# A pool of their own for the MoE's moving tiles, beginning at 64 modulo 128 bytes

## The chip, the cores and the metric

The kernel runs on one core of one Trainium2 chip. The metric is the device time of one execution in microseconds (us), and its median over runs is what versions are compared by. A profiled execution shows every instruction with its start and duration; its span runs from the first instruction to the last.

In the tables, PE is TensorE's matmul stream, PEld its weight loads, DVE is VectorE, ACT is ScalarE, POOL is GpSimd, and SP is the engine whose queue issues the transfers. A phase, in this document, is the start of a tile in its partition's bytes, modulo 128.

## What is computed

A linear attention with a decaying state, and behind it a two-layer network with a leaky rectifier of a slope per channel.

```python
batch, n_heads, seq, head_dim = (4, 8, 768, 48)
for t in range(S):
    cur = einsum('bhd,bhe->bhde', u * k[t], v[t])
    y[t] = einsum('bhd,bhde->bhe', r[t], state + cur)
    state = w * state + einsum('bhd,bhe->bhde', k[t], v[t])
x = y as (3072 tokens, 384)
h = x @ w_in                        # 384 -> 2048
g = maximum(h, 0) + alpha * minimum(h, 0)
out = g @ w_out                     # 2048 -> 384
```

All is float32.

## The kernel before

The sequence is cut into 6 chunks of 128 positions. A chunk of all 4 batches is 512 tokens, the moving width of the network (`NT`). The heads are taken in 4 pairs. The attention of a pair and a chunk is a burst of some hundred small matmuls in float32 (lines 543, 550, 569, 579; the first chunk has its own, 410 to 473): they stream `raw` (the scaled r), `base` (the masked scores) and `v` with 48 or 64 columns, in several parts of the array side by side.

The network (MoE in the code's names) runs over 96 steps, one for each chunk and each of 16 blocks of 128 hidden channels. Its matmuls are in the rounded float32 type, and each factor is split in two, a rounded high part and the rest: `xh`, `xl` for the input, `gh`, `gl` for the hidden values, `wh`, `wl` for the weights. A product is the sum of high by high, high by low and low by high. So a step has 9 matmuls of 128x512 on line 628 (`m_in`: three blocks of 128 input rows, each by the three products) and 9 on line 661 (`m_out`: three products, each into the three output banks `acc`). Between them lie four operations: ScalarE copies the bank to `g` (line 636), VectorE applies the slope (637), ScalarE rounds it to `gh` (640), and VectorE subtracts for `gl` (641). `m_out` of a step runs three steps behind its `m_in` (`MLAG`). In the last product of `m_out` the moving tile is `gl`, and what follows is as a rule the next `m_in`, which begins with `xh` and `wh`. The input tiles are written by lines 361 (`xh`) and 362 (`xl`).

The order of the instructions is fixed when the program is built: `Plan` places each piece by a rank and by modelled durations, and every engine gets its instructions in that order. The addresses have no part in it.

Tiles come from pools that fill a partition from the bottom up, in the order in which the pools are opened, and within a pool by name in the order of first use. The pool `const` holds the tables and all weights, `wk` all else. `sb(shape, name, bufs)` takes a tile from `wk` and gives it a name with so many buffers in rotation. `first_chunk` uses the buffers named `gl` a second time, as its masked scores in every other pair. `seen_y` is a small target that ScalarE writes (line 592) so that it is known when a bank has been written; two of its elements are used.

In the built program before, the phases are: weights `wh` and `wl` 64, `xh`, `xl` and `gh` 64, `gl` 32, `kk`, `rr`, `T` and `wx` 64, `base` and `wraw` 32, `raw` and `g` 0, `v` and `o` 96.

Of the kernel before, what the change touches and what calls it, by code (L numbers as in the profile page):

```python
# [8 lines left out]
F32 = mybir.dt.float32  # L9
# [58 lines left out]
class Plan:  # L68
# [12 lines left out]
    def add(self, eng, us, fn, r=(), w=(), rank=0.0, kb=0.0):  # L81
        p = Piece(eng, us, fn, r, w, rank, kb)
        for ref, wr in p.uses:
            b, part = ref if isinstance(ref, tuple) else (ref, None)
            log = self.log.setdefault(b, [])
            for other, opart, owr in log:
                if other is not p and (wr or owr) and (part is None or opart is None or part == opart):
                    p.after.add(other)
            log.append((p, part, wr))
        self.pieces.append(p)  # L90
        return p
# [85 lines left out]
def rwkv_prelu_kernel(ctx: ExitStack, tc, rk, vkr, wP, uP, u, wall, alpha, w, r_all, k_all, v_all, oT):  # L177
    nc = tc.nc

    const = ctx.enter_context(tc.tile_pool(name="const", bufs=1))  # L180
    pools = ctx.enter_context(ExitStack())
    wk = pools.enter_context(tc.tile_pool(name="wk", bufs=1))
    ps = pools.enter_context(tc.tile_pool(name="ps", bufs=1, space=bass.MemoryType.PSUM))
    part = nc.dram_tensor("part", (2, NK, 128, NT), F32, kind="Internal").ap()
# [3 lines left out]
    plan = Plan()  # L188
    add = plan.add

    def sb(shape, name, bufs, dt=F32):
        return plan.buf(lambda: wk.tile(shape, dt, name=name, bufs=bufs), name, bufs)

    def pb(shape, name, bufs=1):
        return plan.buf(lambda: ps.tile(shape, F32, name=name, bufs=bufs), name, bufs)
# [1 line left out]
    def fixed(shape, name, dt=F32):  # L197
        t = const.tile(shape, dt, name=name)
        return plan.buf(lambda: t)
# [165 lines left out]
    def x_tiles(c, q):  # L365
        if q == 0:
            for t, name in ((xh, "xh"), (xl, "xl")):
                t[c] = sb([128, NK, NT], name, 2, F32R)
                top[name] = sb([112, NT], name + "0", 1, F32R)
        return (top["xh"], top["xl"], None) if q == 0 else (xh[c], xl[c], q - 1)  # L370

# [16 lines left out]
    def first_chunk(q):  # L388
        r, k0 = (sb([112, B, L], *(("o", 2) if q == P - 1 else ("raw", 6))) for _ in range(2))
        v, k = sb([128, 2 * B, D], "v", 4), sb([128, 2 * B, D], "kk", 3)  # L390
        n = 2 * B * D
        inputs(0, q, r, k0, v, k, -99 + 0.1 * q)
        first_k.append(k0)
        first_v.append(v)
        if q == P - 1:
            raw_weights(0, -97, [k0])
            raw_weights(1, -95, [v])
        for j, (t, tab) in enumerate(((r, lambda: W[q]()[:, None, 0:L]), (k0, lambda: W[q]()[:, None, L - 1::-1]))):
            add("DVE", 0.72, lambda t=t, tab=tab: nc.vector.tensor_tensor(
                out=t(), in0=t(), in1=tab().broadcast_to([112, B, L]), op=ALU.mult),  # L400
                r=[W[q]], w=[t], rank=10 * q + j - 90)
        cu = sb([128, 2, B], "cu", 2)
        diagonal(q, r, k0, cu, bank, slice(8 * q, 8 * q + 8), (bank, q), 10 * q - 88, -90.2 + q, -51 + q)

        A = [psum() if q % 2 == 0 else pb([128, NT], f"acc{g}") for g in range(2)]

        def scores():
            for b in range(B):
                for g in range(2):
                    nc.tensor.matmul(A[g]()[:, b * L:(b + 1) * L], k0()[half(g), b], r()[half(g), b], start=(b == 0),  # L410
                                     stop=(b == B - 1), skip_group_check=True)

        add("PE", 1.1, scores, r=[r, k0], w=A, rank=10 * q - 90)
        base = [sb([128, B, L], "gl" if q % 2 else "base", 3) for _ in range(2)]
        for g in range(2):
            for b in range(B):
                add("ACT", 0.39, lambda g=g, b=b: nc.scalar.activation(
                    base[g]()[:, b], ident(), AF.Copy, scale=cu()[:, g, b:b + 1]), r=[cu, ident], w=[(base[g], b)],
                    rank=-50.9 + q)
        for g in range(2):  # L420
            add("DVE", 0.75, lambda g=g: nc.vector.copy_predicated(
                base[g](), strict()[:, None, :].broadcast_to([128, B, L]),
                A[g]()[:, :].rearrange("p (b t) -> p b t", b=B)), r=[strict, A[g]], w=[base[g]],
                rank=10 * q - 76 + g)
        y = psum()

        def out():
            for b in range(B):
                for g in range(2):
                    rows, x = (slice(0, HI) if g == 0 else half(g)), g * B + b  # L430
                    nc.tensor.matmul(y()[rows, b * L:(b + 1) * L], v().rearrange("p x e -> p (x e)")[  # L431
                        :, x * D:x * D + rows.stop - rows.start], base[g]()[:, b], start=b == 0,
                        stop=b == B - 1, skip_group_check=True)

        add("PE", 1.0, out, r=[v] + base, w=[y], rank=10 * q - 90)
        h, l, kx = x_tiles(0, q)
        if q < P - 1:
            splits(kx, h, l, y, lambda: y()[0:112, :], slice(0, 112), slice(0, NT), [0, 2, 3, 4, 5], 0.6, q - 51.2)
        if q:
            lower(0, q - 1)  # L440
        if q == P - 1:
            for g in range(2):
                splits(kx, h, l, y, lambda g=g: y()[half(g), :], half(g), slice(0, NT), [2 + 2 * g, 3 + 2 * g], 0.6,
                       q - 51.2)

        def state():
            load(k, lambda: nc.sync.dma_start(k().rearrange("p x e -> p (x e)"), vkr[0, q, :, n:2 * n]), 192,
                 -20 + q, [first_v[P - 1]])
            U = psum()
            add("DVE", 0.56, lambda: scale_k(k, wtok, q), r=[wtok], w=[k], rank=0.5 * q - 1)  # L450

            def product():
                kt = k().rearrange("p x e -> p (x e)")
                for b in range(B):
                    for g in range(2):
                        rows, x = slice(HI * g, HI if g == 0 else HI + D), g * B + b
                        nc.tensor.matmul(u_rows(U, 0)[rows, b], kt[:, x * D:x * D + rows.stop - rows.start], v()[:, x],
                                         start=(b == 0), stop=(b == B - 1), skip_group_check=True)

            add("PE", 0.8, product, r=[k, v], w=[U], rank=0.5 * q - 1)  # L460
            T[q] = sb([112, B, D], "T", 9)
            add("ACT", 0.4, lambda t=T[q]: nc.scalar.activation(t(), u_rows(U, 0), AF.Copy), r=[U], w=[T[q]],
                rank=0.5 * q - 1)
        return state
# [13 lines left out]
            cu(), sums()[:, cols].rearrange("p (b g) -> p g b", g=2), AF.Copy), r=[mine], w=[cu], rank=copy_rank)  # L478


    seen_y = fixed([1, 2], "seen_y")
    pairs = [(c, q) for c in range(1, C) for q in range(P)]
    made = {}

# [39 lines left out]
    def burst(i, was, at):  # L524
# [64 lines left out]
        first = add("PE", (0.7 if before else 0.1) + (0.8 if now else 0.1), run, r=uses, w=writes, rank=at)  # L589
        if before:  # L590

            seen = add("ACT", 0.2, lambda: nc.scalar.activation(seen_y(), y[1]()[0:1, L + HI - 1:L + HI + 1], AF.Copy),
                       r=[y[1]], rank=at - 200)
            seen.soon[first] = 0.75
            add("PE", 0.3, lambda: through_scores(1), r=[v0, base0], w=y, rank=at - 200)
# [26 lines left out]
    def m_in(n):  # L622
        c, i = STEPS[n]
        hp = psum("hp", 2)
        for k in range(NK):
            def mm(k=k):
                for j, (a, x) in enumerate(((wh, xh), (wl, xh), (wh, xl))):
                    nc.tensor.matmul(hp()[:, :], a[i]()[:, k], x[c]()[:, k], start=(k == 0 and j == 0),  # L628
                                     stop=(k == NK - 1 and j == 2))

            need = range(NK) if c and k == 0 else (k,)
            add("PE", 0.7, mm, r=[wh[i], wl[i]] + [(t[c], (kx, p)) for t in (xh, xl) for kx in need for p in range(6)],
                w=[hp], rank=n)
        g = sb([128, NT], "g", 3)
        gh, gl = sb([128, NT], "gh", 3, F32R), sb([128, NT], "gl", 3, F32R)
        add("ACT", 0.6, lambda: nc.scalar.activation(g(), hp()[:, :], AF.Copy), r=[hp], w=[g], rank=n - 100)  # L636
        add("DVE", 0.75, lambda: nc.vector.scalar_tensor_tensor(  # L637
            out=g(), in0=hp()[:, :], scalar=alph()[:, i:i + 1], in1=g(), op0=ALU.mult, op1=ALU.max), r=[hp, alph], w=[g],
            rank=n - 100)
        add("ACT", 0.64, lambda: nc.scalar.activation(gh(), g(), AF.Copy), r=[g], w=[gh], rank=n - 100)  # L640
        add("DVE", 0.73, lambda: nc.vector.tensor_tensor(out=gl(), in0=g(), in1=gh(), op=ALU.subtract), r=[g, gh],  # L641
            w=[gl], rank=n - 99)
        gs[n] = gh, gl
# [256 lines left out]
```

## Time and profile before

| | us |
|---|---|
| median of 3 runs | 502.45 |
| least and most of the 3 | 500.54, 502.52 |
| the profiled execution | 498.5 |
| its span, first to last instruction | 496.7 |
| TensorE busy in the span | 477.7 |
| VectorE, ScalarE, GpSimd busy | 322.1, 242.5, 45.1 |

The page divides the span into 40 slices of 12.4 us and gives a digit for each: the share of the slice in tenths in which an engine was busy, and for PEclk the clock that TensorE was granted, in tenths of full speed. A matmul's duration in the profile overlaps the next one's, since matmuls are pipelined; from one start to the next is the time that it holds the array.

### The profile page before, as it was taken

What the parts mean: (1) busy time and instruction counts of PE and PEld (TensorE: products, weight loads), DVE (VectorE), ACT (ScalarE), POOL (GpSimd) and SP (SyncE); (2) the same over time, 40 slices, a digit from 0 to 9 for tenths busy, and PEclk for the clock granted to TensorE, in tenths of its full rate; (3) what the DMA queues carried; (4) which work ended last, traced back from release to release, by engine and by line L of the source; (5) the groups of instructions that cost most, each with busy time, mean ns of one, the idle gap of its engine ahead of it and who ended that gap; (6) DMA issues with size and microseconds to landing.
All of it is one profiled execution on the core that took longest, in us unless ns stands there. A gap on an engine that the chain in (4) does not pass through costs nothing.

```text
span 496.7 us, 11103 instructions
## 1 busy us (share of the span) xinstructions
PE 477.7 (96%) x4563; PEld 390.2 (79%) x4563; DVE 322.1 (65%) x550; ACT 242.5 (49%) x565; POOL 45.1 (9%) x49
## 2 busy tenths in 40 slices
PE   7989878999999999999999999999999999999994
PEld 6857756788888888888888888888888878888883
DVE  7799999999986677656647546747535434333331
ACT  3777557666764455535535635535633333423332
POOL 2000100001312112100311101211000000000000
PEclk9799999999999999999999999999999999999998
DMA  7965575374152253413212213312120000100001
GB/s 220 299 172 189 153 226 196 126 233 161 49 189 90 80 169 100 147 43 83 86 36 86 95 56 84 86 36 70 63 54 1 1 1 1 64 0 2 0 1 68
DMA packets 24888, 47.39 MB, mean 95 GB/s; under 512 B 4096, under 2 KB 12416, under 8 KB 24832
## 3 DMA queue, kind: packets, MB, share of 16 engines
q1 hardware_dynamic: 24832, 46.62, 30.3%
q8 instruction: 38, 0.62, 0.5%
q14 instruction: 18, 0.15, 0.1%
HBM read 37.96 MB, written 6.29 MB: 89 GB/s over the span
## 4 chain that ended last, share of the span: by engine, by line
PE 84%; DVE 8%; ACT 3%; DMA 2%; issue 1%; SPq 0%; DVEq 0%; ACTq 0%
PE acc L661 38%; PE bank L628 36%; PE bank L569 2%; PE bank L579 2%; PE bank L550 2%; PE bank L543 2%; DMA wraw<-wall 1%; DVE wx L333 1%; DVE xl L362 1%; DMA raw<-rk 1%; DVE wl L337 1%; DVE wx L330 1%; DVE g L637 1%; PE acc L473 1%; DVE raw L496 1%
## 5 line engine op out<-in xcount | busy, mean ns | idle before, releaser
L637 DVE SCALAR_TENSOR_TENSOR g<-bank,alph,g 128x512 f32<-128x512 f32 x96 | 72.0, 750 | 110.0 <-ACT g L636 108.5
L636 ACT ACTIVATE g<-bank 128x512 f32<-128x512 f32 x96 | 57.3, 597 | 141.0 <-PE bank L628 139.1
L628 PE MATMUL bank<-xh,wh 128*128 128x512 f32 x288 | 113.6, 395 | 3.4 <-DVE T L605 3.4
L628 PE MATMUL bank<-xh,wl 128*128 128x512 f32 x288 | 112.3, 390 | 0.4 <-DVE wl L337 0.3
L628 PE MATMUL bank<-xl,wh 128*128 128x512 f32 x288 | 112.1, 389 | 0.0
L640 ACT ACTIVATE gh<-g 128x512 fp32r<-128x512 f32 x96 | 60.6, 632 | 71.3 <-DVE g L637 71.1
L641 DVE TENSOR_TENSOR gl<-g,gh 128x512 fp32r<-128x512 f32 x96 | 70.0, 730 | 37.1 <-ACT gh L640 37.0
L661 PE MATMUL acc<-gh,wh 128*128 128x512 f32 x288 | 83.6, 397 | 1.6 <-ACT gh L640 1.6
L661 PE MATMUL acc<-gl,wh 128*128 128x512 f32 x288 | 83.2, 396 | 0.0
L661 PE MATMUL acc<-gh,wl 128*128 128x512 f32 x288 | 81.7, 391 | 0.0
L628 PEld LDWEIGHTS bank<-xh,wh 128*128 128x128 f32 x288 | 54.1, 188 | 15.8 <-ACT wx L326 3.8
L628 PEld LDWEIGHTS bank<-xh,wl 128*128 128x128 f32 x288 | 54.1, 188 | 12.6 <-DVE wl L337 1.3
L661 PEld LDWEIGHTS acc<-gl,wh 128*128 128x128 f32 x288 | 54.1, 188 | 12.1
L628 PEld LDWEIGHTS bank<-xl,wh 128*128 128x128 f32 x288 | 54.0, 188 | 11.7
L661 PEld LDWEIGHTS acc<-gh,wl 128*128 128x128 f32 x288 | 53.9, 188 | 11.6
L661 PEld LDWEIGHTS acc<-gh,wh 128*128 128x128 f32 x288 | 52.6, 188 | 13.2 <-ACT gh L640 1.9
L507 POOL TENSOR_TENSOR rr<-rr,kk 128x384 f32<-128x384 f32 x16 | 21.4, 1337 | 294.9 <-DMA kk<-vkr 155.8
L518 ACT ACTIVATE base<-ident,cu 128x64 f32<-128x64 f32 x160 | 41.4, 337 | 1.1 <-DVE cu L513 1.0
L362 DVE TENSOR_TENSOR xl<-bank,xh 48x256 fp32r<-48x256 f32 (+2 forms) x85 | 37.2, 438 | 3.5 <-ACT xh L361 1.7
L361 ACT ACTIVATE xh<-bank 48x256 fp32r<-48x256 f32 (+2 forms) x85 | 33.3, 392 | 7.8 <-PE bank L431 3.4
L496 DVE TENSOR_TENSOR raw<-raw,W 112x512 f32<-112x512 f32 x40 | 26.3, 681 | 0.3 <-DMA raw<-rk 0.3
L509 POOL TENSOR_TENSOR rr<-rr,utab 128x384 f32<-128x384 f32 x16 | 21.0, 1310 | 1.3
(93 smaller groups left out, 375.1 us busy)
## 6 DMA issues: line engine op xcount, KB each, us to landing
wraw<-wall SPq DMA_DIRECT2D x16, 768.0 KB, 4.8
raw<-rk SPq DMA_DIRECT2D x46, 224.0 KB, 4.2
v<-vkr SPq DMA_DIRECT2D x24, 192.0 KB, 4.0
kk<-vkr SPq DMA_DIRECT2D x24, 192.0 KB, 3.6
rr<-vkr SPq DMA_DIRECT2D x16, 192.0 KB, 2.4
oT<-o SPq DMA_DIRECT2D x12, 256.0 KB, 2.1
oT<-g SPq DMA_DIRECT2D x6, 256.0 KB, 2.6
xh<-xh SPq DMA_DIRECT2D x36, 32.0 KB, 2.5
```

What stands on the lines that cost most here:

```text
L361: add("ACT", us, lambda: nc.scalar.activation(to(h), view(), AF.Copy), r=[src], w=refs(h), rank=rank)
L362: add("DVE", us + 0.1, lambda: nc.vector.tensor_tensor(out=to(l), in0=view(), in1=to(h), op=ALU.subtract), r=[src] + refs(h), w=refs(l), r ...
L496: add("DVE", 0.72, lambda t=t, tab=tab: nc.vector.tensor_tensor(out=t().rearrange("p b (j t) -> p (b j) t", j=2), in0=t().rearrange("p b ( ...
L507: add("POOL", 1.2, lambda: nc.gpsimd.tensor_tensor(out=rt(), in0=rt(), in1=k(), op=ALU.mult), r=[k] + ([wh[12]] if c == 2 else []), w=[rt] ...
L509: add("POOL", 1.2, lambda: nc.gpsimd.tensor_tensor(out=rt().rearrange("p (g b) e -> p g b e", g=2), in0=rt().rearrange("p (g b) e -> p g b ...
L518: add("ACT", 0.32, lambda g=g, b=b: nc.scalar.activation(base()[:, g, b], ident2(), AF.Copy, scale=cu()[:, g, b:b + 1]), r=[cu, ident2], w ...
L628: nc.tensor.matmul(hp()[:, :], a[i]()[:, k], x[c]()[:, k], start=(k == 0 and j == 0), stop=(k == NK - 1 and j == 2))
L636: add("ACT", 0.6, lambda: nc.scalar.activation(g(), hp()[:, :], AF.Copy), r=[hp], w=[g], rank=n - 100)
L637: add("DVE", 0.75, lambda: nc.vector.scalar_tensor_tensor(out=g(), in0=hp()[:, :], scalar=alph()[:, i:i + 1], in1=g(), op0=ALU.mult, op1=A ...
L640: add("ACT", 0.64, lambda: nc.scalar.activation(gh(), g(), AF.Copy), r=[g], w=[gh], rank=n - 100)
L641: add("DVE", 0.73, lambda: nc.vector.tensor_tensor(out=gl(), in0=g(), in1=gh(), op=ALU.subtract), r=[g, gh], w=[gl], rank=n - 99)
L661: nc.tensor.matmul(banks[k](), a[i]()[:, NK + k], x(), start=(begin and j == 0), stop=(end and j == 2))
```

## The change

A pool `mv` is opened between `const` and `wk`, and the tiles named `xh`, `xl`, `gh` and `gl` are taken from it, the second use of `gl` in the first chunk with them. `seen_y` becomes 24 elements wide in place of 2, of which the same two are used: `const` then ends at byte 121664 of a partition, and `mv` begins there, at 64 modulo 128. On every engine the instructions of the program's main part, their order and their waits are the same as before.

```diff
+    mv = pools.enter_context(tc.tile_pool(name="mv", bufs=1))
     wk = pools.enter_context(tc.tile_pool(name="wk", bufs=1))
...
-    def sb(shape, name, bufs, dt=F32):
-        return plan.buf(lambda: wk.tile(shape, dt, name=name, bufs=bufs), name, bufs)
+    def sb(shape, name, bufs, dt=F32, pool=None):
+        return plan.buf(lambda: (pool or wk).tile(shape, dt, name=name, bufs=bufs), name, bufs)
...
-                t[c] = sb([128, NK, NT], name, 2, F32R)
+                t[c] = sb([128, NK, NT], name, 2, F32R, mv)
...
-        base = [sb([128, B, L], "gl" if q % 2 else "base", 3) for _ in range(2)]
+        base = [sb([128, B, L], "gl", 3, F32, mv) if q % 2 else sb([128, B, L], "base", 3) for _ in range(2)]
...
-    seen_y = fixed([1, 2], "seen_y")
+    seen_y = fixed([1, 24], "seen_y")
...
-            seen = add("ACT", 0.2, lambda: nc.scalar.activation(seen_y(), y[1]()[0:1, L + HI - 1:L + HI + 1], AF.Copy),
+            seen = add("ACT", 0.2, lambda: nc.scalar.activation(seen_y()[:, 0:2], y[1]()[0:1, L + HI - 1:L + HI + 1], AF.Copy),
...
-        gh, gl = sb([128, NT], "gh", 3, F32R), sb([128, NT], "gl", 3, F32R)
+        gh, gl = (sb([128, NT], name, 3, F32R, mv) for name in ("gh", "gl"))
```

The phases in the built program (start of a tile in a partition, modulo 128):

| tiles | before | after |
|---|---|---|
| `wh`, `wl` | 64 | 64 |
| `xh`, `xl`, `gh` | 64 | 64 |
| `gl` | 32 | 64 |
| `raw`, `g` | 0 | 64 |
| `kk`, `rr`, `T`, `wx` | 64 | 0 |
| `base`, `wraw` | 32 | 96 |
| `v`, `o` | 96 | 32 |

## Rows read from the trace of the kernel before

**Rows 1.** The page's busy times by engine, and its slices for TensorE and for the granted clock.
```profile
PE 477.7 (96%) x4563; PEld 390.2 (79%) x4563; DVE 322.1 (65%) x550; ACT 242.5 (49%) x565; POOL 45.1 (9%) x49
...
PE   7989878999999999999999999999999999999994
...
PEclk9799999999999999999999999999999999999998
```

**Rows 2.** The page's chain of work that ended last, by engine and by line.
```profile
PE 84%; DVE 8%; ACT 3%; DMA 2%; issue 1%; SPq 0%; DVEq 0%; ACTq 0%
PE acc L661 38%; PE bank L628 36%; PE bank L569 2%; PE bank L579 2%; PE bank L550 2%; PE bank L543 2%; DMA wraw<-wall 1%; DVE wx L333 1%; DVE xl L362 1%; DMA raw<-rk 1%; DVE wl L337 1%; DVE wx L330 1%; DVE g L637 1%; PE acc L473 1%; DVE raw L496 1%
```

**Rows 3.** One stretch, from 60 to 490 us: its length, busy time and instructions of each engine, granted clock, share of the DMA engines, GB/s.
```profile
60.00:490.00 430.00, 425.06 (x3976) 347.99 (x3974) 269.85 (x451) 203.98 (x461) 42.35 (x32) 1.00 0.25 78
```

**Rows 4.** The instructions of single tiles on TensorE, for `gl`, `gh`, `xh` and `xl`: least, median and longest duration in ns, first and last start in us, and the shape.
```profile
L661 PE MATMUL acc<-gl,wh x288: 388/397/398, 42.9 to 489.7; 128*128 128x512 f32 x144
...
L661 PE MATMUL acc<-gh,wh x288: 387/389/501, 41.5 to 489.3; 128*128 128x512 f32 x144
L661 PE MATMUL acc<-gh,wl x288: 387/389/511, 42.2 to 489.5; 128*128 128x512 f32 x144
...
L628 PE MATMUL bank<-xh,wh x288: 388/389/504, 31.2 to 483.1; 128*128 128x512 f32 x144
...
L628 PE MATMUL bank<-xl,wh x288: 387/389/397, 31.8 to 483.5; 128*128 128x512 f32 x144
```

**Rows 5.** TensorE's groups of instructions between 420 and 480 us, where no burst runs: count, busy us, mean ns of one, idle time before them.
```profile
L628 PE MATMUL bank<-xh,wh 128*128 128x512 f32 x45 | 17.6, 391 | 0.0
...
L628 PE MATMUL bank<-xl,wh 128*128 128x512 f32 x45 | 17.5, 389 | 0.0
L661 PE MATMUL acc<-gl,wh 128*128 128x512 f32 x44 | 12.7, 396 | 0.0
```

**Rows 6.** TensorE's matmuls in order of time, from two stretches: start, us, operation, count where equal ones follow each other. The last row is from the program's last step, where a matmul with `gh` comes right behind one with `gl`.
```profile
430.35 0.84 PE L661 MATMUL acc<-gh,wh 128*128 128x512 f32 x3
431.03 0.84 PE L661 MATMUL acc<-gh,wl 128*128 128x512 f32 x3
431.71 0.86 PE L661 MATMUL acc<-gl,wh 128*128 128x512 f32 x3
432.41 0.40 PE L628 MATMUL bank<-xh,wh 128*128 128x512 f32 x1
...
433.09 0.39 PE L628 MATMUL bank<-xh,wh 128*128 128x512 f32 x1
...
435.81 0.86 PE L661 MATMUL acc<-gl,wh 128*128 128x512 f32 x3
...
487.86 0.40 PE L661 MATMUL acc<-gh,wh 128*128 128x512 f32 x1
```

**Rows 7.** The chain of work in order of time, in the same stretch: start, us, what. Between the first two rows and the last one the pieces alternate without another one between them.
```profile
424.36 2.04 PE bank L628 x9
426.40 2.06 PE acc L661 x9
...
481.85 2.04 PE bank L628 x9
```

**Rows 8.** The instructions of the tiles `raw`, `base` and `o` on TensorE, columns as in rows 4.
```profile
L550 PE MATMUL bank<-raw x640: 218/218/330, 40.1 to 391.2; 48*64 48x64 f32 x160
L569 PE MATMUL bank<-raw,T x640: 216/216/311, 50.6 to 408.7; 48*48 48x64 f32 x160
...
L410 PE MATMUL acc<-raw x16: 272/272/419, 11.7 to 12.7; 48*128 48x128 f32 x16
...
L579 PE MATMUL bank<-base,v x640: 213/215/311, 51.1 to 410.2; 64*48 64x64 f32 x160
...
L410 PE MATMUL acc<-o x16: 272/272/373, 21.3 to 22.2; 48*128 48x128 f32 x16
```

**Rows 9.** Groups of instructions over the whole span, columns as in rows 5: the two of the bursts that stream `raw`.
```profile
L550 PE MATMUL bank<-raw 48*64 48x64 f32 x640 | 15.3, 226 | 0.0
...
L569 PE MATMUL bank<-raw,T 48*48 48x64 f32 x640 | 13.9, 225 | 0.1
```

**Rows 10.** The same view for VectorE: one operation on two tiles each.
```profile
L399 DVE TENSOR_TENSOR raw<-raw,W 112x512 f32<-112x512 f32 x6 | 4.0, 688 | 1.3 <-DMA raw<-rk 1.3
...
L685 DVE TENSOR_TENSOR o<-acc,o 128x512 f32<-128x512 f32 x4 | 2.7, 687 | 0.2 <-PE acc L661 0.2
...
L399 DVE TENSOR_TENSOR o<-o,W 112x512 f32<-112x512 f32 x2 | 1.4, 684 | 0.0
L685 DVE TENSOR_TENSOR g<-acc,g 128x512 f32<-128x512 f32 x2 | 1.4, 681 | 0.0
```

**Rows 11.** The page's DMA issues: count, KB each, median us from issue to landing.
```profile
raw<-rk SPq DMA_DIRECT2D x46, 224.0 KB, 4.2
...
kk<-vkr SPq DMA_DIRECT2D x24, 192.0 KB, 3.6
...
oT<-o SPq DMA_DIRECT2D x12, 256.0 KB, 2.1
oT<-g SPq DMA_DIRECT2D x6, 256.0 KB, 2.6
```

**Rows 12.** The chain in order of time, from its first 34 us: the transfer in it.
```profile
2.68 4.56 DMA raw<-rk
```

**Rows 13.** TensorE's matmuls in order of time, one group of a burst: start, us, count.
```profile
409.97 0.44 PE L579 MATMUL bank<-base,v 64*48 64x64 f32 x16
```

## The prediction

> **What bounds the kernel now.** I read the page's busy times and slices first: TensorE is busy 96% of the span, and from the eighth slice (87 us) on at nine tenths or more in each but the last, with the granted clock at full in all but the first two slices and the last [rows 1]. The second view is the chain of work that ended last: 84% of it is TensorE, and 74% are two lines, 661 (the second product of the MoE, `m_out`) and 628 (the first, `m_in`) [rows 2]. The third is the stretch from 60 to 490 us by itself: TensorE works 425 of 430 us at the full clock, VectorE 270, ScalarE 204 [rows 3]. So there the time is the sum of the intervals from one matmul to the next, and the other engines have room. What matters then is how long one matmul holds the array, and whether an address can have a part in that.
>
> **What the addresses are.** Of the four names that move, three stood at 64 modulo 128 before (`xh`, `xl`, `gh`), as all weights do; `gl` alone stood at 32. The change brings `gl` from 32 to 64, leaves the phase of the other three as it was, and shifts the phase of nearly everything in `wk` that it doesn't name: `raw` and `g` from 0 to 64, `kk`, `rr`, `T` and `wx` from 64 to 0, `base` and `wraw` from 32 to 96, `v` and `o` from 96 to 32. So there are two questions: what `gl` paid at 32, and whether anything pays at its new place.
>
> **Term 1, gl's matmuls.** The MoE has six products that differ in their moving tile and weight, all 128x512 by the same instruction. Five are in [rows 4]: four of them have a median of 389 ns, the one that streams `gl` has 397. In a stretch without bursts the means say the same: 389 for `xl`, 396 for `gl`, and 391 for `xh` with `wh` [rows 5]. Those durations are modelled in part, so I check them with starts. In order of time, three `gh,wh` take 0.68 us from start to start (430.35 to 431.03), three `gh,wl` the same (to 431.71), three `gl` 0.70 (to 432.41). From 433.09 to 435.81 twelve matmuls without `gl` take 2.72 us, 226.7 ns each [rows 6]. The matmul right behind the last `gl` is long too: 0.40 us at 432.41 against 0.39 for the same product at 433.09, which is why `xh,wh` has a mean of 391. The longest clean ruler is the chain in order of time: from 424.36 to 481.85 lie 14 steps, each nine matmuls of line 628 and nine of line 661 [rows 7]. That is 57.49 / 14 = 4.106 us a step, where 18 matmuls at 226.7 ns would be 4.081. The surcharge is 0.026 us a step (by pieces, 0.02 for the three `gl` and about 0.006 for the one behind). Over 96 steps that is 96 x 0.026 = **2.5 us**. By durations it would be 288 x 8 ns = 2.3 and, for the one behind, 96 x 6 = 0.6, so 2.9 at the upper end; by the three `gl` alone, if the follower is late for another reason, 96 x 0.02 = 1.9.
>
> Is it the address? `xl` is the last product of its triple too, uses `wh`, is written by VectorE by the same kind of subtraction, and is at 389. `gh` goes to the same three banks with the same weights and is at 389. What is left that sets `gl` apart is its start at 32, where the others start at 64. All steps but the first few, ahead of 60 us, lie on TensorE's path, so nearly the whole sum reaches the end. The engines that make `gl` get no faster, but `m_out` runs three steps behind `m_in` (some 12 us), and a step that is shorter by 0.026 doesn't use that up. I take 2.5.
>
> The Trainium skill, page "SBUF — State Buffer", section Specifications, has lines of 16 bytes in this memory and a price for each crossing to a new line; 32 and 64 both begin such a line, and a row of 2048 bytes has 128 of them from either. By that rule alone the change is worth 0 and the time stays 502.45. Rows 4 don't agree with it, since 397 and 389 stand side by side.
>
> **Term 2, the other matmuls.** The attention's matmuls read `raw` (as moving tile and as weights), `base`, `v`, `kk` and `T`, in float32 and not in the rounded type. The trace has phases side by side: the scores of the first chunk read `raw` at 0 and `o` at 96 in one shape, and both have 272 ns at best and in the median; in the bursts `base` at 32 has a median of 215, `raw` at 0 has 218 and 216 [rows 8]. Phase costs these nothing that the rows show, and I take 0. A bound: the two groups of the bursts that stream `raw` are busy 15.3 and 13.9 us [rows 9]; a surcharge of `gl`'s share, 8 in 389 or 2%, on these 29.2 us would be 0.6. The same share the other way would be a gain, since no row has `raw` at 64. So plus or minus 0.6.
>
> **Term 3, VectorE, ScalarE and the loads.** The same operation at two phases: `raw` at 0 and `o` at 96 times the table, 688 and 684 ns; `o` at 96 and `g` at 0 in the last sum, 687 and 681 [rows 10]. All within 1%, and after 60 us beside TensorE's work. That cover is gone in the first 30 us, where the chain has such work; 1% of 30 us is 0.3, either way. Taken as 0.
>
> Of the transfers, `raw` goes from a multiple of 256 to one of 64. Two stores read `o` at 96 and `g` at 0 and take 2.1 and 2.6 us to landing for 256 KB; two loads take 4.2 us for 224 KB into `raw` at 0 and 3.6 for 192 KB into `kk`, which starts at 64, 18.75 ns per KB in either [rows 11]. No price shows, and I take 0. On the path lies one such load, 4.56 us at the start [rows 12]. The Trainium skill, page "DMA: Bandwidth & Descriptors", section "How a descriptor splits into AXI transactions", has a read that doesn't start at a multiple of 256 bytes cost one more transaction. If that held for the side that is written, a row of 2048 bytes would have 9 in place of 8, an estimate by that page of 4.56 / 8 = 0.6 us more and a gain of 1.9; rows 11 don't bear it out.
>
> **Sum.** The profiled execution took 498.5 us, of which 496.7 is the span: 498.5 - 2.5 = 496.0, with a span of 494.2. That execution lies 4 us below the median of the three runs, 502.45, and 2 below the least, 500.54; nothing in the change speaks to that difference, so I carry the term over: 502.45 - 2.5 = **499.95 us**.
>
> **Rivals.**
> - *No effect: `gl` is slow for its place in the order.* Its three matmuls are the last of `m_out`. Against it: the last product of `m_in`, `xl`, is at 389, and the matmul behind `gl` is long whether it belongs to line 628 (0.40 at 432.41) or to line 661 (0.40 at 487.86) [rows 6]. Time: 502.45.
> - *Half of it.* The start at 32 is only part of the surcharge, and the rest belongs to the switch from one written tile to the next. 1.2 us are gained: 501.2.
> - *Slower: `raw` at 64.* Its rows of 256 bytes in the bursts began at a multiple of 128 before; now each touches three pieces of 128 in place of two. If the array pays by such pieces, the 1280 records of lines 550 and 569 pay. At `gl`'s 8 ns a record that is 10.2 us if nothing overlaps; they do overlap (16 records of the burst's kind take 0.44 us where one lasts 215 ns [rows 13], so eight are in flight), and if only every second pays visibly, 5.1. Less the 2.5 gained: 2.6 slower, 505.05. It decides from 2.5 / 1280 = 2 ns a record. Against it: `gh` and `xh` start at 64 and are the fastest of their kind, and `o` at 96, which touches one piece more as well, costs what `raw` at 0 does [rows 8].
> - *The change doesn't do what it says.* The pool begins at byte 121664 of a partition, 64 modulo 128, and each tile in it is a multiple of 128 long; excluded by the layout.
>
> **How the numbers follow.** Chances: 0.78 for the forecast, 0.09 for no effect, 0.06 for half, 0.07 for slower. The forecast's own range is its bounds (1.9 to 2.9 gained, 0.6 either way in term 2) and the scatter of three runs that span 2 us: 498.7 to 501.3. The cases at 501.2 and 502.45 belong to the range of 8 in 10; the slower one is left out: **498.7 to 502.7**. About half a percent, 2.5 us, is what a measurement of this kernel can tell from no change, and the forecast lies on that line, at 0.498%. Of its 0.78 I give 0.40 to faster by over 0.5% and 0.38 to within it; with no effect and half, within is 0.53. Slower by over 0.5% is 0.07.
>
> **What would show it.** In the profile after: `acc<-gl,wh` at a median of 389; `xh,wh` at the mean of its neighbours; a step of 4.08 us in the stretch without bursts, in place of 4.106; TensorE as busy from 60 us on as before. Wrong if `gl` stays at 397 (no effect), if `gl` falls and the step keeps part of its 0.026 (half), or if lines 550 and 569 rise above 218 and 216 (slower). If the step is 4.08 and the time doesn't fall, the time was lost ahead of 60 us, where loads and VectorE's work are on the chain.

## The result, and the profile after

| | before | after |
|---|---|---|
| median of 6 runs, us | 500.89 | 506.70 |
| least and most, us | 498.92, 502.52 | 504.76, 508.17 |
| the profiled execution, us | 498.5 | 507.59 |
| its span, us | 496.7 | 505.8 |

The ratio is 1.011, with an interval of [1.0075, 1.0147]: slower by 1.1%, where a gain of 2.5 us was forecast. The profiled execution of after lies near the top of its six, that of before below the bottom of its own, so their distance of 9.1 us is more than the medians' 5.8.

The instructions of single tiles on TensorE, after (least, median and longest ns, first and last start), answer to [rows 4]:

```profile
L662 PE MATMUL acc<-gl,wh x288: 388/393/404, 45.3 to 499.0; 128*128 128x512 f32 x144
...
L662 PE MATMUL acc<-gh,wh x288: 390/393/503, 43.9 to 498.6; 128*128 128x512 f32 x144
L662 PE MATMUL acc<-gh,wl x288: 390/393/499, 44.6 to 498.8; 128*128 128x512 f32 x144
...
L629 PE MATMUL bank<-xh,wh x288: 390/395/774, 28.5 to 492.3; 128*128 128x512 f32 x144
...
L629 PE MATMUL bank<-xl,wh x288: 387/395/628, 29.1 to 492.7; 128*128 128x512 f32 x144
```

`gl` has come down from 397 to 393, but from start to start its three take 0.70 us as before (431.37 to 432.07 below, against 431.71 to 432.41 in [rows 6]). But `gh`, `xh` and `xl`, which I had left alone because their phase modulo 128 stayed at 64, went up from 389 to 393 and 395. The least of `gh` is now 390, above the old median: not some of them are slow, all are.

The chain in order of time, after, in the stretch without bursts, against [rows 7]:

```profile
425.93 2.10 PE acc L662 x9
428.03 2.10 PE bank L629 x9
...
484.73 2.10 PE acc L662 x9
```

From 425.93 to 484.73 lie 14 steps: 4.200 us each, where before had 4.106. Both lines have 2.10 for nine, 233.3 ns a matmul. TensorE's matmuls in order of time show the shape of it (columns as in [rows 6]):

```profile
431.37 0.86 PE L662 MATMUL acc<-gl,wh 128*128 128x512 f32 x3
...
432.07 0.40 PE L629 MATMUL bank<-xh,wh 128*128 128x512 f32 x1
432.07 0.19 PEld L629 LDWEIGHTS bank<-xh,wl 128*128 128x128 f32 x1
432.31 0.39 PE L629 MATMUL bank<-xh,wl 128*128 128x512 f32 x1
432.31 0.19 PEld L629 LDWEIGHTS bank<-xl,wh 128*128 128x128 f32 x1
432.54 0.40 PE L629 MATMUL bank<-xl,wh 128*128 128x512 f32 x1
...
432.77 0.39 PE L629 MATMUL bank<-xh,wh 128*128 128x512 f32 x1
...
433.00 0.40 PE L629 MATMUL bank<-xh,wl 128*128 128x512 f32 x1
```

The durations alternate, 0.40 and 0.39, whichever tile it is: the stream of matmuls has fallen into a pattern of two. And each weight load begins with the matmul ahead of the one that it is for (432.31 and 432.31): while one matmul streams its moving tile, the next one's weights are read.

Most of the 9.1 us lie in these matmuls. The starts of the first and the last `base` matmul of the bursts, in the row below, and of the last `gl`, in the first row above, cut the span (against [rows 8] and [rows 4]):

```profile
L580 PE MATMUL bank<-base,v x640: 213/215/253, 52.9 to 417.8; 64*48 64x64 f32 x160
```

From the first burst to the last it took 359.1 us before and 364.9 after, from there to the last `gl` 79.5 and 81.2: 7.5 us together. Another 1.8 were lost ahead of 52.9 us, and the end behind the last `gl` was 0.2 shorter. TensorE had been busy for 2.2 of the 5.4 us from 28.5 to 33.9, with the chain on a transfer into `xh`; then the granted clock fell to its lower level, 1.2 GHz (0.50 of full speed from 33.9 to 38.1 us, where before had 1.00; before was low at another place, with 0.55 from 12 to 18 us). By then the MoE had begun, and nine matmuls took twice their time. In the chain in order of time of after:

```profile
33.92 4.18 PE bank L629 x9
```

That is where the clock fell in this one execution, and I don't count it to the change: e4 below has the pool too, and its first `base` matmul of the bursts starts at 50.3 us, ahead of before's 51.1. The attention's matmuls did not move: `raw` has the medians of [rows 8], 218 and 216, at its new phase too:

```profile
L551 PE MATMUL bank<-raw x640: 218/218/330, 41.8 to 398.6; 48*64 48x64 f32 x160
L570 PE MATMUL bank<-raw,T x640: 216/216/254, 52.4 to 416.3; 48*48 48x64 f32 x160
```

### The profile page after: what moved, and what is told of

It is laid out like the page before. It is cut to its first block, busy times and chain, and to the rows that moved or that the text cites. A ratio compares the mean times of both kernels' runs of the same rounds, so it can differ in the third digit from the quotient of the medians.

```text
span 505.8 us, 11103 instructions
## 1 busy us (share of the span) xinstructions
PE 484.8 (96%) x4563; PEld 391.2 (77%) x4563; DVE 325.0 (64%) x550; ACT 243.0 (48%) x565; POOL 43.4 (9%) x49
## 4 chain that ended last, share of the span: by engine, by line
PE 85%; DVE 5%; ACT 3%; DMA 3%; SPq 1%; issue 1%; ACTq 0%; DVEq 0%
PE bank L629 39%; PE acc L662 38%; PE bank L570 2%; PE bank L551 2%; PE bank L580 2%; PE bank L544 2%; DMA wraw<-wall 1%; ACT base L418 1%; ACT gl L418 1%; DMA xh<-xh 1%; DVE wx L334 1%; DMA raw<-rk 1%; DVE wl L338 1%; DVE xl L363 1%; DVE raw L497 1%
## 5 line engine op out<-in xcount | busy, mean ns | idle before, releaser
L629 PE MATMUL bank<-xh,wh 128*128 128x512 f32 x288 | 116.8, 406 | 6.5 <-DVE T L606 5.0
L629 PE MATMUL bank<-xh,wl 128*128 128x512 f32 x288 | 115.1, 400 | 0.1
L629 PE MATMUL bank<-xl,wh 128*128 128x512 f32 x288 | 115.0, 399 | 0.0
L662 PE MATMUL acc<-gh,wh 128*128 128x512 f32 x288 | 84.9, 402 | 1.8 <-ACT gh L641 1.8
L662 PE MATMUL acc<-gh,wl 128*128 128x512 f32 x288 | 83.1, 395 | 0.0
L629 PEld LDWEIGHTS bank<-xh,wh 128*128 128x128 f32 x288 | 55.2, 192 | 19.9 <-ACT wx L327 5.4
L629 PEld LDWEIGHTS bank<-xl,wh 128*128 128x128 f32 x288 | 55.1, 191 | 13.4 <-DMA xl<-xl 0.2
L629 PEld LDWEIGHTS bank<-xh,wl 128*128 128x128 f32 x288 | 55.4, 192 | 13.0 <-DVE wl L338 0.5
L599 DVE COPY_PREDICATED base<-strict,bank 128x256 f32<-128x256 uint8 x40 | 15.7, 443 | 6.3 <-PE bank L551 6.3
```

Of the source, the lines that this page charges most:

```text
L599: add("DVE", 0.42, lambda g=g: nc.vector.copy_predicated(base()[:, g], strict2()[:, None, :].broadcast_to([128, B, HI]), A[g]()[:, 0:256]. ...
L662: nc.tensor.matmul(banks[k](), a[i]()[:, NK + k], x(), start=(begin and j == 0), stop=(end and j == 2))
```

## The experiments

**The question.** What slowed tiles whose start modulo 128 is the same? Counted modulo 256 it is not the same: before, `xh`, `xl`, `gh` and all weights stood at 192, `gl` at 160; after, all four moving tiles stand at 64 and the weights still at 192. Three theories: R, a moving tile's start counts against the weights' start, modulo 256; A, its own start counts; N, it is the new neighbourhood, low in the partition, with other tiles moved around it.

The edits are a pad each. The width of `seen_y`, the last tile ahead of the pool, sets where the pool begins.

```diff
# e1_mv192: after, moving tiles at 192 modulo 256
-    seen_y = fixed([1, 24], "seen_y")
+    seen_y = fixed([1, 56], "seen_y")
# e2_both64: after, a table of 128 bytes behind the weights, which so stand at 64
-    strict = fixed([128, 128], "strict", U8)
...
     flag = fixed([1, 1], "flag", I32)
+    strict = fixed([128, 128], "strict", U8)
# e3_before_plus128: the kernel before, 128 bytes more ahead of its one pool
-    seen_y = fixed([1, 2], "seen_y")
+    seen_y = fixed([1, 40], "seen_y")
...
-            seen = add("ACT", 0.2, lambda: nc.scalar.activation(seen_y(), y[1]()[0:1, L + HI - 1:L + HI + 1], AF.Copy),
+            seen = add("ACT", 0.2, lambda: nc.scalar.activation(seen_y()[:, 0:2], y[1]()[0:1, L + HI - 1:L + HI + 1], AF.Copy),
# e4_both0: after, both at 0
+    padw = fixed([1, 16], "padw")
     wh, wl = ...
...
-    seen_y = fixed([1, 24], "seen_y")
+    seen_y = fixed([1, 56], "seen_y")
```

> The new kernel with 128 bytes more ahead of the pool: all moving tiles start at 192 modulo 256, as the weights do (the new kernel has 64 against 192, the kernel before 192 against 192 but for gl at 160). Theory R (what counts is the moving tile's start against the weights' start, modulo 256): every matmul goes back to 226.7 ns from start to start, gl's too, a step of 4.08 us, 2.5 us faster than the kernel before (ratio 0.995). Theory A (the moving tile's own start, 192 good and 64 bad): the same here. Theory N (the new neighbourhood: moving tiles low in the partition, other tiles moved): 231 to 238 ns as in the new kernel, ratio 1.011.

> The new kernel with the weights 128 bytes lower (a table of 128 bytes moved from ahead of them to behind them): weights and moving tiles both at 64 modulo 256, and no moving tile or working tile at another address than in the new kernel. Theory R: 226.7 ns everywhere, ratio 0.995 against the kernel before. Theory A: as the new kernel, some 233 ns and ratio 1.011. Theory N: the same, 1.011.

> The kernel before, with one pool, and 128 bytes more ahead of it: xh, xl and gh at 64 modulo 256 against weights at 192, gl at 32. No tile is in another pool. Theories R and A: slow like the new kernel, about 233 ns and ratio 1.011 or worse. Theory N: as the kernel before, 226.7 ns with gl's surcharge, ratio 1.000.

> Weights and moving tiles both at 0 modulo 256. Theory R: 226.7 ns, ratio 0.995, as e1. If an even start helps by itself (the rows are then whole pieces of 256), the interval falls below 226.7, at best to the 213 ns that 512 columns take at 2.4 GHz: ratio down to 0.95. Theory A: 0 is neither 192 nor 64; open. Theory N: 1.011.

Measured against the kernel before on the same chip (25 runs, 499.96 us): e1 497.94 us, 0.9952 [0.9914, 0.9991]; e2 497.69, 0.9953 [0.9923, 0.9983]; e3 506.45, 1.0117 [1.006, 1.0173]; e4 498.76, 0.9991 [0.9954, 1.0028]. The chain in order of time, e1, then e2, then e3:

```profile
424.79 2.04 PE acc L662 x9
426.83 2.04 PE bank L629 x9
...
485.99 2.04 PE acc L662 x9
```

```profile
424.25 2.04 PE bank L629 x9
...
481.37 2.04 PE bank L629 x9
```

```profile
426.67 2.10 PE bank L628 x9
...
485.47 2.10 PE bank L628 x9
```

e1: 61.20 / 15 = 4.080 us a step, 226.7 ns a matmul, no surcharge left anywhere. e3: 58.80 / 14 = 4.200. R is the one that holds. e2 speaks against A and N: no moving tile and no working tile stands elsewhere than in the slow kernel, only the weights and the small tables ahead of them do, which no matmul of the MoE reads, and the step is 4.080 (424.25 to 481.37, 14 steps). e3 speaks against N from the other side: one pool, the old order, and as slow as after, with `gl` 96 bytes ahead of the weights and the other three 128 away. e4 has the same step of 4.080 (424.24 to 481.36); a start at a multiple of 256 for both gives nothing more, and its ratio, whose interval overlaps e1's, doesn't contradict the step. e1 and e2 are faster than both kernels.

**Is an equal start the best?** The other distances, weights left at 192, by the width of `seen_y` in after (e5 8, e6 64, e7 48, e8 40, e10 16, e11 32 in place of 24).

> Moving tiles at 0, weights at 192 modulo 256: 64 bytes ahead of the weights. Theory R1 (equal starts are best, every other distance pays): 232 to 235 ns a matmul, ratio 1.010 to 1.015 against the kernel before. Theory R2 (equal starts still meet at the same pieces of the memory, and a distance that is neither 0 nor 128 meets less): below 226.7 ns, at best 213, ratio 0.95 to 0.99.

> Moving tiles 32 bytes ahead of the weights (224 against 192). R1: 232 to 235 ns as gl had at 32 behind, ratio 1.010 to 1.015; if the price rises with the distance, less than at 64. R2: below 226.7 ns, ratio under 0.99.

> Moving tiles 64 bytes behind the weights (128 against 192). R1: 232 to 235 ns, ratio 1.010 to 1.015. R2: below 226.7. If ahead and behind differ, it differs from the run with 64 ahead.

> All moving tiles 32 bytes behind the weights (160 against 192), as gl alone was in the kernel before. If each mismatched matmul pays by itself, all pay what gl paid, 233 to 235 ns, ratio 1.010 to 1.018. If gl's price came from the switch between equal and unequal starts, less: 227 to 230, ratio up to 1.005.

> Moving tiles 96 bytes ahead of the weights (32 against 192). So far: 0 ahead 226.9 ns, 32 ahead 233.3, 64 ahead 229.0, 128 ahead 232.7, 64 behind 233.3. If multiples of 64 ahead are milder than odd multiples of 32, 232 to 235 here, ratio 1.010 to 1.018; if ahead is milder than behind up to 128, 229 to 231, ratio 1.004 to 1.008. Below 226.7 would be a better start than an equal one.

> Moving tiles 96 bytes behind the weights (96 against 192). By the neighbours (64 behind 233.3, 128 either way 232.7): 232 to 235 ns, ratio 1.010 to 1.018. Below 226.7 would be a better start than an equal one.

Each ratio is to runs of the kernel before on the same chip: 13 with a median of 500.24 us for e5, e6, e8 and, below, e9; 7 with 500.13 for e7, e10, e11 and, below, e12. The 226.9, 229.0 and 232.7 ns that the expectations name for 0, +64 and 128 are 226.7, 228.9 and 233.3 by the chain.

| moving start less weights' start | run | step, us (chain, from, to, steps) | ns a matmul | ratio to before |
|---|---|---|---|---|
| 0 | e1 | 4.080 | 226.7 | 0.9952 [0.9914, 0.9991] |
| +32 | e6 | 4.200 (423.13, 486.13, 15) | 233.3 | 1.0174 [1.013, 1.0218] |
| +64 | e5 | 4.120 (423.91, 485.71, 15) | 228.9 | 1.0038 [1.0007, 1.0068] |
| +96 | e10 | 4.200 (423.13, 486.13, 15) | 233.3 | 1.0174 [1.0125, 1.0224] |
| 128 | after | 4.200 | 233.3 | 1.0111 [1.0075, 1.0147] |
| -96 | e11 | 4.217 (425.35, 484.39, 14) | 234.3 | 1.0170 [1.0132, 1.0208] |
| -64 | e8 | 4.200 (423.33, 486.33, 15) | 233.3 | 1.0138 [1.0083, 1.0193] |
| -32 | e7 | 4.200 (422.00, 485.00, 15) | 233.3 | 1.0179 [1.0132, 1.0227] |

R1 holds: an equal start is best, and no distance goes below 226.7 ns. Every other one pays 6 to 8 ns but +64, which pays 2, in a pattern of three matmuls (229, 232 and 226 ns by the starts in e5's trace), where 232 to 235 had been expected. Why 64 ahead is milder than 64 behind isn't settled. The ratios at -32, +32, +96 and -96 are up to 0.007 above that of after at equal or nearly equal steps, and the intervals overlap. Part of it lies in the stretches with bursts: by the starts in the traces from 150 to 400 us (without the first matmul behind each burst), one MoE matmul to the next takes 232.4 ns in after, 233.2 to 233.4 at -32, +32 and +96, and 234.3 at -96. What is left of it stays open.

**Whose weights?** Only `wl` at another start, and only `gh` and `gl`.

```diff
# e9_wl64: wh and all moving tiles at 192, wl at 64
-    wh, wl = ([fixed([128, 2 * NK, 128], f"{n}{i}", F32R) for i in range(NF)] for n in ("wh", "wl"))
+    wh = [fixed([128, 2 * NK, 128], f"wh{i}", F32R) for i in range(NF)]
+    padw = fixed([1, 32], "padw")
+    wl = [fixed([128, 2 * NK, 128], f"wl{i}", F32R) for i in range(NF)]
# e12_split: xh and xl in a pool behind mv, with a pad of 128 bytes: at 192; gh and gl stay at 64
+    mx = pools.enter_context(tc.tile_pool(name="mx", bufs=1))
...
-                t[c] = sb([128, NK, NT], name, 2, F32R, mv)
+                t[c] = sb([128, NK, NT], name, 2, F32R, mx)
...
+    padx = mx.tile([1, 32], F32, name="padx")
```

> All moving tiles and wh at 192, wl alone at 64. If a matmul pays for its own weights' start against its own moving tile: xh,wl and gh,wl (a third of all) pay 6 ns, 227 for the rest, and the time is 576 x 6 ns = 3.5 us above the run with all at 192, ratio 1.002. If a matmul pays for the weights that are loaded while it streams, which are the next one's: the same sum, but on those ahead of a wl: xh,wh, the third gh,wh of a step and the first two gh,wl, with xh,wl and xl,wh at 227.

> The input's tiles xh and xl at 192, equal to the weights; gh and gl at 64 as in the new kernel. If the price is paid matmul by matmul, nine of 18 pay: the first product's line at 226.7 ns but for the one behind a gl, the second product's line at 232 to 234, a step of 4.13 to 4.15 us, and the ratio lies between the run with all at 192 (0.995) and the new kernel (1.011), near 1.003. If one mismatch anywhere throws the stream off for good, both lines are at 232 to 234 and the ratio is 1.011.

e9: 506.11 us, 1.0136 [1.009, 1.0181], a step of 4.167 (422.62 to 485.12, 15 steps). TensorE's matmuls in order of time:

```profile
432.19 0.85 PE L664 MATMUL acc<-gl,wh 128*128 128x512 f32 x3
432.88 0.40 PE L631 MATMUL bank<-xh,wh 128*128 128x512 f32 x1
...
433.58 0.40 PE L631 MATMUL bank<-xh,wh 128*128 128x512 f32 x1
433.58 0.19 PEld L631 LDWEIGHTS bank<-xh,wl 128*128 128x128 f32 x1
433.81 0.40 PE L631 MATMUL bank<-xh,wl 128*128 128x512 f32 x1
433.81 0.19 PEld L631 LDWEIGHTS bank<-xl,wh 128*128 128x128 f32 x1
434.04 0.39 PE L631 MATMUL bank<-xl,wh 128*128 128x512 f32 x1
...
434.27 0.40 PE L631 MATMUL bank<-xh,wh 128*128 128x512 f32 x1
...
435.65 0.87 PE L664 MATMUL acc<-gh,wl 128*128 128x512 f32 x3
...
436.36 0.39 PE L664 MATMUL acc<-gl,wh 128*128 128x512 f32 x1
```

The sum that I expected, 3.5 us over e1, was less than half of it: (4.167 - 4.080) x 96 = 8.4. `xh,wh` is long although its own weights stand equal: it streams while the `wl` of the next is read. So its own weights alone are not what counts. `xh,wl` behind it is long too, although the `wh` that is read meanwhile stands equal; only the third is back at 0.39. In `m_in` the mismatch costs the matmul that streams across it, and the one behind. In `m_out` it costs more: the three `gh,wl` take 0.71 us (435.65 to 436.36), 236.7 ns each, above any row of the table, and the three `gl,wh` behind such ones, at equal starts, 0.69 (432.19 to 432.88) against 0.68. So neither of the two expected forms holds as it stands.

e12: 504.85 us, 1.0103 [1.0057, 1.0149], a step of 4.160 (423.65 to 486.05, 15 steps):

```profile
433.90 0.39 PE L631 MATMUL bank<-xh,wh 128*128 128x512 f32 x1
...
434.13 0.40 PE L631 MATMUL bank<-xh,wl 128*128 128x512 f32 x1
...
434.60 0.40 PE L631 MATMUL bank<-xh,wh 128*128 128x512 f32 x1
...
435.29 0.39 PE L631 MATMUL bank<-xh,wh 128*128 128x512 f32 x1
435.29 0.19 PEld L631 LDWEIGHTS bank<-xh,wl 128*128 128x128 f32 x1
435.51 0.39 PE L631 MATMUL bank<-xh,wl 128*128 128x512 f32 x1
...
435.74 0.39 PE L631 MATMUL bank<-xl,wh 128*128 128x512 f32 x1
```

From 433.90 to 435.29 the six first matmuls of `m_in`, all at equal starts, take 1.39 us, some 231 ns each; from 435.29 to 435.74 two take 0.45, which fits 226.7 each to the hundredth that is shown. So it is neither matmul by matmul (4.13 to 4.15 expected) nor for good (4.200): the stream comes back by itself, in about six matmuls. Half of the tiles at an equal start gained a third of the step's difference, (4.200 - 4.160) / (4.200 - 4.080). The ratio alone doesn't show it: 1.0103 can't be told from after's 1.0111.

The same return stands in e1 behind a burst, where all starts are equal:

```profile
227.63 0.96 PE L662 MATMUL acc<-gh,wh 128*128 128x512 f32 x3
228.43 0.85 PE L662 MATMUL acc<-gh,wl 128*128 128x512 f32 x3
229.12 0.84 PE L662 MATMUL acc<-gl,wh 128*128 128x512 f32 x3
229.80 0.39 PE L629 MATMUL bank<-xh,wh 128*128 128x512 f32 x1
```

Behind the first three the next three take 0.69 us (228.43 to 229.12), and only those after them 0.68. So a burst throws the stream off too; at equal starts it settles again, and at the other distances in the table it doesn't, even in stretches of 60 us without a burst.

## Why the prediction was wrong

**The step that failed** is the one headed "What the addresses are": "three stood at 64 modulo 128 before (`xh`, `xl`, `gh`), as all weights do", and the change "leaves the phase of the other three as it was". The change was described modulo 128, and the working took that over; what `xh`, `xl` and `gh` cost was put at unchanged for that reason alone. Modulo 256 the three had stood where the weights stand, and the change took them off by 128. From there the sum had one term, a gain for `gl`, which didn't come, since `gl` too now stands 128 from the weights; and it lacked a loss for 15 of a step's 18 matmuls.

**Term 1** read the trace rightly: `gl` paid for its address, and 0.026 us a step was its price. e1, which brings `gl` to the weights' start and keeps the other three there, gains 0.026 a step (4.106 - 4.080) and 2.4 us by its ratio of 0.9952, where I had 2.5. What was wrong is why: 32 was bad for being 32 bytes behind the weights, not for not being 64. The rows couldn't tell the two apart, since they had `gl` at one start and the rest at one other; that no row showed a moving tile at 64 modulo 256 should have been asked for all four, as I asked it for `raw`.

**Of the rivals**, "slower" had the right side and the wrong tile: 505.05 was close to the 506.7 measured, but `raw` at its new phase kept 218 and 216. "No effect" and "half of it" are out by e1's step of 4.080, in which the whole 0.026 is gone. **Term 2** held as a sum: the float32 matmuls kept their medians at the new starts. It says less than it seems, though: the tiles that the bursts' matmuls read all lie in `wk` and moved by the same 64 bytes, so the distance from a moving tile to its weights, which is what counted in the MoE, stayed as it was, and the rows on `raw` and `o` compare two starts at one distance. **Term 3** was not what decided; the load at the start of the chain took 4.36 us, no longer than in [rows 12], and the 1.8 us ahead of 52.9 us lie where the clock fell.

**What it comes to.** Of 18 matmuls in a step 15 went from 226.7 to 233.3 ns; the three with `gl` had been at some 233 already. By steps that is 96 x (4.200 - 4.106) = 9.0 us; in the stretches with bursts the two kernels are nearer to each other (228.5 ns from one MoE matmul to the next before and 232.4 after, by the starts from 150 to 400 us), and from the first burst to the last `gl` the traces differ by 7.5. The medians differ by 5.8, with an interval from 3.8 to 7.4. What remains between 7.5 and 5.8 I can't separate from the scatter.

Two rules of the Trainium skill are touched. The page "SBUF — State Buffer", section "Specifications (TRN2)", has lines of 16 bytes and a price for each crossing to a new one. The runs show something that this rule doesn't give: all eight starts in the table begin such a line, and they differ by up to 7.6 ns in 226.7. The page "TensorE: Matmul & The Clock Gate", section "Step-by-step: what each phase is for", has two independent read ports, one for the moving operand and one for the weights. The runs show that the two operands are not independent in time: by after and e2 the same moving tiles at the same addresses take 233.3 or 226.7 ns a matmul by where the weights lie. What makes one operand's start matter to the other, and why 256 bytes, these runs don't show.

## What to carry to other kernels

Where matmuls of a full 512 rounded-float32 columns run back to back, each with its own weight load, lay the moving tiles and the weights at the same start modulo 256 bytes: here it was worth some 2% between the worst distance (1.018) and the best (0.995), for one pad. A change of any pool's size moves every tile behind it, so print the starts of both operands after each such change, and compare them modulo more than the number that the change speaks of. A tile that is slow beside its like shows that a start matters, not which start is right; that takes a second address.

## What the runs showed of the hardware that was not expected

- The interval of back-to-back matmuls with 512 columns depends on the distance of the two operands' starts modulo 256: 226.7 ns at 0, 228.9 at +64, 233.3 to 234.3 at the six others that are multiples of 32. It is 256 and not 512: before, `xh` stood 256 from the weights modulo 512, `gh` at 0, and both have 389 ns in [rows 4].
- It belongs to the stream more than to one matmul: the durations fall into patterns of two (after) or three (e5), and after a mismatch (e12) or a burst (e1) it takes about six matmuls at equal starts to be back at 226.7.
- The float32 matmuls of the attention show no price of their own start (medians of 218, 216 and 215 before and after). Whether the distance to their weights matters to them isn't shown: no run changed it in the bursts.
